# Turning the second product round: weights stationary, 448 tokens moving, output transposed, and two late terms

## The chip, the cores and the metric

The kernel runs on one core of a Trainium2 chip. The metric is the device time of one launch in microseconds; three runs gave 1165.35 to 1166.55, median 1165.88.

The core's engines work from queues of their own: PE (TensorE, the matmuls; PEld is its loading of weights), DVE (VectorE), ACT (ScalarE), POOL (GpSimd) and SP (SyncE, which issues most DMAs). An engine works through its queue in the order in which the instructions were written, and they wait for each other by semaphores. Each core has a small memory PSUM, into which matmuls add up; its banks are handed out from pools.

## The reference

Attention with a sigmoid in place of the softmax, then a product with `w_in`, a function of each element, and a product with `w_out`:

```python
scores = scale * np.matmul(q, k.transpose(0, 1, 3, 2)) - np.log(S)
attn = 1.0 / (1.0 + np.exp(-scores))
x = np.matmul(attn, v)          # (8, 12, 448, 64), then x: (3584, 768)
h = x @ w_in                    # (768, 2048)
g = h - np.tanh(h)
out = g @ w_out                 # (2048, 768)
```

There are 8 batches of 448 tokens (S) and 12 heads of width 64. All inputs and the output are f32.

## The kernel before

Work goes by batches. For each batch there is attention for 12 heads in six pairs (method `stream`, L467 on: scores `sc`, L394; the sigmoid on ACT, `a`, L405; its split into two f16 parts, `ahl`, L411 on ACT and L412 on DVE; the product with v, `acc`, L425; its move to `x`, L437 or L439), then the first product (`moe1`, `ph`, L773) with the function `g` behind it, and the second product (`moe2`, L838). To keep the accuracy of f32 with f16 matmuls, an operand is split into a high and a low f16 part, and a product is the sum of three (`prods`: high x high, high x low, low x high).

The attention of batch b + 1 runs among the matmuls of the second product of batch b. For b of 1 and above the method `second` does this: `moe2` is a generator that yields after each f (one of 16 slices of 128 rows of `w_out`), and the list BLOCKS says behind how many such steps the next block of attention is written. The numbers 16, 32 and 48 are the ends of token tiles. Batch 1 has a list of its own (BLOCKS1) with the same number 16. For batch 0 the order is written out by hand: a string ORDER with one letter for each piece, in which P is a piece of the second product. There the weights `w_out` are still being loaded (`rawo`), measured (`stb` on ACT, L170, then the matmuls `wl`, L201), scaled and split (`wo`, L237 and L240) at the same time.

The second product before: `gs` holds g with its 2048 rows on partitions, so 128 tokens of it are the stationary operand and half of `w_out` (384 columns) moves. A batch has three tiles of 128 tokens with two halves each (288 matmuls of 384 columns, `po`, L857), and then 64 tokens left over (`por`, L905: 96 matmuls with 64 stationary columns, two of which go to the two halves of a bank's partitions). Finished tiles are scaled by `iK` and moved to `o` by ACT (L890; in batch 0 `oh`, L876) and DVE (L894), for one tile by ACT alone (L892), the remainder by DVE (`orem`, L914), and stored by SP (L850). The PSUM pool `mm` has two banks, and a new tile waits until the eviction of the tile that had its bank is done.

Of the kernel before, what the change touches and what calls it, by code (L numbers as in the profile page):

```python
# [10 lines left out]
F32 = mybir.dt.float32  # L11
# [3 lines left out]
AF = mybir.ActivationFunctionType  # L15
ALU = mybir.AluOpType
# [3 lines left out]
P = 128  # L20
D = 64
# [12 lines left out]
class Builder:  # L34
# [5 lines left out]
    ORDER = (  # L40
        "lurmlorumsrrsrrmmlussmvvrrssvvrlrssvvrrvruvlssrurssvvrrssvlrrsvvvursrsvs"
        "vrrssvrsrrvvvvRrRrRRRMrRRRnRrRRGMRRwtMttRtRBtwRRtMwBgttMtRtRttMBttRtRttM"
        "tMBBtRttRMtBttMttMtRxtRtBRAtMtttAMtBttMttAttAttMMtAtPPtaRPRBPtBbtCaBCBAC"
        "PtFCCPBPCPPBZPPPCSBCPPBZCBCPPCCBPCCCSZBPPCCCPCXBaaAPaPPPBAPPaaaBBSPPSPSZ"
        "PSZSPPPPPPPSPBPPPZPPPNPZPSPZPSSNNPPSZPPZSSPPPPPPPPPPPP"
    )

    BLOCKS = (8, 11, 16, 20, 20, 20, 27, 32, 36, 36, 36, 43, 48, 52, 52)
# [242 lines left out]
    def w_out_scale(self, e):  # L291

        V = self.nc.vector
        self.w_out_bound(e)
        m = self.bound[e]
        total = self.sm.tile([P, 1], F32, name="wtot2")
        V.scalar_tensor_tensor(total, m, 1.05, m, op0=ALU.mult, op1=ALU.mult)
        S, inv = self.scale_of(total, f"swo{e}")
        self.Swo.append(S)
        V.tensor_copy(self.iSwo[:, e : e + 1], inv)  # L300
        h = slice(e * D, (e + 1) * D)
        V.tensor_copy(self.iSwo[h, 2:3], inv[h])

    def split_w_out(self, e):
        for f in range(0, self.NF, 2):
# [531 lines left out]
    def moe2(self, b, gs):  # L837
        nc = self.nc  # L838
        S = self.S
        ks = self.ks  # L840
        iK = self.sm.tile([P, 3], F32, name="iK")
        n = 1 if b == 0 else 3
        nc.vector.tensor_scalar(iK[:, :n], self.iSwo[:, :n], self.iSg, None, op0=ALU.mult)
        H = self.HALF
        base = b * S
        prods = ((0, 0), (0, 1), (1, 0))
        last = (self.NF - 1, 2)

        def store(o, j0, n, cols, queue=nc.sync):
            queue.dma_start(self.out[base + j0 : base + j0 + n, cols], o)  # L850

        nt = S // P

        def products(po, tk, f, e):
            for n, (x, w) in enumerate(prods):
                for i in e:
                    nc.tensor.matmul(  # L857
                        po[i][:, :H],
                        gs[f // 2][:, x, f % 2, tk * P : (tk + 1) * P],
                        self.wo[:, i * self.NF + 2 * ks[f // 2] + f % 2, w],  # L860
                        start=(f == 0 and n == 0),
                        stop=((f, n) == last),
                    )

        if b == 0:
            for e in range(2):
                for tk in range(nt):
                    po = {e: self.ps.tile([P, 512], F32, name="po", tag="mm", bufs=2)}
                    for f in range(0, self.NF, 2):
                        products(po, tk, f, (e,))  # L870
                        products(po, tk, f + 1, (e,))
                        if f + 2 == self.NF:
                            if (e, tk) == (1, 0):
                                nc.vector.tensor_scalar(iK[:, 1:], self.iSwo[:, 1:], self.iSg, None, op0=ALU.mult)
                            o = self.op.tile([P, H], F32, name="oh", tag="o", bufs=2)
                            nc.scalar.activation(o, po[e][:, :H], AF.Copy, scale=iK[:, e : e + 1])  # L876
                            store(o, tk * P, P, slice(e * H, (e + 1) * H))
                        yield 980
        else:
            for tk in range(nt):  # L880
                if b + 1 == self.B and tk % 2:
                    both = self.ps.tile([P, 2, 512], F32, name="po", tag="sc", bufs=2)
                    po = [both[:, e] for e in range(2)]
                else:
                    po = [self.ps.tile([P, 512], F32, name=f"po{e}", tag="mm", bufs=2) for e in range(2)]
                for f in range(self.NF):
                    products(po, tk, f, (0, 1))
                    if f == self.NF - 1:
                        o = self.op.tile([P, self.DM], F32, name="o", tag="o", bufs=2)
                        nc.scalar.activation(o[:, :H], po[0][:, :H], AF.Copy, scale=iK[:, 0:1])  # L890
                        if (b, tk) == (1, 0):
                            nc.scalar.activation(o[:, H:], po[1][:, :H], AF.Copy, scale=iK[:, 1:2])  # L892
                        else:
                            nc.vector.tensor_scalar(o[:, H:], po[1][:, :H], iK[:, 1:2], None, op0=ALU.mult)  # L894
                        store(o, tk * P, P, slice(0, self.DM))
                    yield 980
        nm = nt * P
        if b + 2 < self.B:
            po = self.ps.tile([P, 512], F32, name="por", tag="mm", bufs=2)
        else:  # L900
            po = self.ps.tile([P, 2, 512], F32, name="por", tag="sc", bufs=2)[:, 0]
        for f in range(self.NF):
            for n, (x, w) in enumerate(prods):
                for e in range(2):
                    nc.tensor.matmul(  # L905
                        po[e * D : (e + 1) * D, :H],
                        gs[f // 2][:, x, f % 2, nm:S],
                        self.wo[:, e * self.NF + 2 * ks[f // 2] + f % 2, w],
                        start=(f == 0 and n == 0),
                        stop=((f, n) == last),  # L910
                    )
            yield 560
        o = self.op.tile([P, H], F32, name="orem", tag="o", bufs=2)
        nc.vector.tensor_scalar(o, po[:, :H], iK[:, 2:3], None, op0=ALU.mult)  # L914
        for e in range(2):
            queue = nc.scalar if e and b + 1 == self.B else nc.sync
            store(o[e * D : (e + 1) * D], nm, S - nm, slice(e * H, (e + 1) * H), queue)


    def build(self):  # L920
        nc, tc = self.nc, self.tc

        def const(name, value, n=1):
            t = self.const.tile([P, n], F32, name=name)
            nc.vector.memset(t, value)
            return t

        self.nls = const("nls", -math.log(self.S))
        self.b1 = const("b1", B1)
        self.b2 = const("b2", B2)  # L930
        self.b3 = const("b3", -CUT * CUT)
        self.tiny = const("tiny", TINY)
        self.ih0 = const("ih0", 1.0)
        self.ihk0 = const("ihk0", KAPPA)
        self.iSwo = const("iswo", 1.0, 3)
        self.sums = [const(f"ss{i}", 0.0, 6) for i in range(2)]
        self.Swo = []
        self.sums_out, self.bound = [[], []], [None, None]
        self.xs32, self.x2b = False, []
        pieces = list(self.pieces())  # L940
        nA = 4 * self.NC
        E = mybir.EngineType
        with tc.manual_schedule(engines={E.PE, E.Activation, E.DVE, E.Pool}):
            nB = nA + self.NF + self.EARLY
            self.stage = tc.alloc_tile_pool(name="stage", bufs=2, reuse_waits="tile")
            self.blocks = self.stream()
            self.first(
                self.convert(pieces[:nA], "attention"),
                self.convert(pieces[nA:nB], "mixture"),
                self.convert(pieces[nB:], "product"),  # L950
            )
        with tc.manual_schedule(engines={E.PE, E.Activation, E.DVE, E.Pool, E.SP}):
            for b in range(1, self.B):
                self.batch(b)
        self.gp.release()
# [128 lines left out]
    def second(self, b, blocks, alone, events):  # L1084

        step = lambda: next(self.blocks)
        events += [(p, step) for p in blocks]
        scales = []

        def norms():  # L1090
            scales.append(self.batch_scales(self.xs, False))
            next(scales[0])

        if blocks:
            end = blocks[alone]
            events.append((end + 3, norms))
            events += [(p, lambda: next(scales[0], None)) for p in (end + 5, end + 7)]
        events.sort(key=lambda e: e[0])
        full = self.NF * (self.S // P)
        for k, _ in enumerate(self.moe2(b, self.gs)):  # L1100
            now = k + 1 if k < full else full + (k + 1 - full) / 2
            while events and events[0][0] <= now:
                events.pop(0)[1]()
        assert not events
# [34 lines left out]
```

## Time and profile before

| | |
|---|---|
| Median of the three runs | 1165.88 us |
| The profiled execution | 1166.29 us |
| Its span, first to last instruction | 1164.5 us |
| PE busy | 1153.1 us |
| DVE busy | 907.7 us |
| ACT busy | 865.5 us |
| Idle of PE in front of `po` (L857) | 3.1 us in all |
| Mean granted TensorE clock | 0.999 |

Busy times are those of one execution. The profile's chain of work follows the execution back from its last instruction, at each step to what released it; its pieces add up to the span. In the timeline a row is a run of instructions of one kind with its start, its length, the engine, the line, and in brackets the idle time in front of it with what ended it. Matmuls overlap in their pipeline, so the time of one in the queue is that of a long run divided by its count.

### The profile page before, as it was taken

Reading aid. Unit: us, or ns where it says so; the run is one execution under the profiler, and the core shown is the slowest. Engines: PE = TensorE matmul, PEld = TensorE weight load, DVE = VectorE, ACT = ScalarE, POOL = GpSimd, SP = SyncE. Lnnn points to the kernel's source line nnn. Section 1 sums busy time; section 2 is a strip of 40 time slices with the busy share of each in tenths; the row PEclk is TensorE's granted clock in tenths of the full one; section 3 lists DMA queues with packets and bytes.
Section 4 is the critical chain, followed back from the end, with each engine's and each line's share of the span. In section 5 each row is a group of like instructions: output and inputs, shape, how many; then the busy total and the mean of one; then the engine's idle time right before and its main releaser. Section 6 shows DMA issues by size and latency. Waiting matters only on the chain.

```text
span 1164.5 us, 18896 instructions
## 1 busy us (share of the span) xinstructions
PE 1153.1 (99%) x7563; PEld 597.4 (51%) x7564; DVE 907.7 (78%) x1308; ACT 865.5 (74%) x1195; POOL 79.1 (7%) x58
## 2 busy tenths in 40 slices
PE   9999999999999999999999999999999999999998
PEld 3345444555555555555555555555555555555565
DVE  6999999789777996679867897778976798646930
ACT  7988996588976888768887688867887688745820
POOL 0000000000120002200021000200022000300000
PEclk9999999999999999999999999999999999999999
DMA  9942171000222002210022101210012100000000
GB/s 358 357 163 64 42 224 53 29 7 1 80 75 64 7 1 78 62 53 1 17 76 62 40 1 31 82 58 24 1 55 84 53 1 9 23 28 7 1 14 35
DMA packets 34056, 70.43 MB, mean 60 GB/s; under 512 B 3888, under 2 KB 21040, under 8 KB 33968
## 3 DMA queue, kind: packets, MB, share of 16 engines
q1 hardware_dynamic: 33744, 68.89, 18.1%
q8 instruction: 59, 0.97, 0.4%
q10 hardware_dynamic: 224, 0.33, 0.1%
q14 instruction: 29, 0.24, 0.1%
HBM read 58.20 MB, written 11.01 MB: 59 GB/s over the span
## 4 chain that ended last, share of the span: by engine, by line
PE 73%; ACT 1%; issue 0%; DVE 0%; ACTq 0%
PE ph L773 28%; PE po L857 27%; PE sc L394 6%; PE acc L425 6%; PE por L905 5%; ACT a L405 0%; ACT ahl L411 0%; PE nm L690 0%; ACT sqn L335 0%; ACT x L439 0%; ACT Q L369 0%; DVE orem L914 0%; PE pbn L344 0%; ACT x L454 0%; ACT o L892 0%
## 5 line engine op out<-in xcount | busy, mean ns | idle before, releaser
L857 PE MATMUL po<-wo,g 128*128 128x384 f16 x2304 | 389.1, 326 | 3.1 <-DVE wo L240 1.6
L773 PE MATMUL ph<-xhl,wi 128*128 128x448 f16 x2016 | 382.6, 352 | 0.0
L857 PEld LDWEIGHTS <-g 128*128 128x128 f16 x2304 | 220.3, 98 | 170.1 <-issue 26.4
L773 PEld LDWEIGHTS <-wi 128*128 128x128 f16 x2016 | 196.7, 98 | 185.0 <-issue 2.1
L412 DVE SCALAR_TENSOR_TENSOR ahl<-a,ahl 128x896 f16<-128x896 f32 x126 | 162.7, 1326 | 125.6 <-ACT ahl L411 125.0
L405 ACT ACTIVATE a<-sc,nls,rn 128x896 f32<-128x896 f32 x147 | 155.8, 1090 | 37.4 <-PE sc L394 37.2
L811 ACT ACTIVATE u<-ph,ih 128x896 f32<-128x896 f32 x64 | 64.4, 1006 | 75.8 <-PE ph L773 74.0
L411 ACT ACTIVATE ahl<-a 128x896 f16<-128x896 f32 x126 | 113.2, 941 | 0.6
L394 PE MATMUL sc<-Q,K 64*128 64x448 f16 x1008 | 100.8, 353 | 0.9 <-DVE th L816 0.7
L815 DVE SCALAR_TENSOR_TENSOR m<-ph,ihk,u 128x896 f32<-128x896 f32 x64 | 73.5, 1149 | 25.6 <-ACT th L813 25.2
L766 ACT ACTIVATE g<-m,Sg 128x896 f16<-128x896 f32 x64 | 66.7, 1041 | 35.5 <-DVE m L829 28.5
L829 DVE COPY_PREDICATED m<-u,th 128x896 f32<-128x896 uint32 x64 | 77.2, 1206 | 6.8 <-ACT u L828 0.8
L425 PE MATMUL acc<-ahl,vhl 128*64 128x448 f16 (+1 forms) x864 | 80.6, 356 | 0.4 <-ACT tn L346 0.4
L456 POOL TENSOR_TENSOR x<-x 128x448 f32<-128x448 f32 x24 | 28.3, 1178 | 762.1 <-ACT x L439 762.1
L767 DVE SCALAR_TENSOR_TENSOR g<-m,Sg,g 128x896 f16<-128x896 f32 x64 | 73.4, 1147 | 6.8 <-ACT g L766 6.7
L826 DVE SCALAR_TENSOR_TENSOR m<-q,m 128x896 f32<-128x896 f32 x64 | 69.9, 1092 | 6.7 <-DVE m L822 0.5
L983 PE MATMUL ph<-x,wi 128*128 128x448 f32 x192 | 73.8, 540 | 0.0
L816 DVE SCALAR_TENSOR_TENSOR th<-ph,ih,th 128x896 f32<-128x896 f32 x64 | 73.3, 1145 | 0.0
L822 DVE SCALAR_TENSOR_TENSOR m<-q,m 128x896 f32<-128x896 f32 x64 | 69.6, 1087 | 0.0
L828 ACT ACTIVATE u<-u,b 128x896 f32<-128x896 f32 x64 | 66.7, 1042 | 1.9
L821 ACT ACTIVATE q<-u,b 128x896 f32<-128x896 f32 x64 | 65.8, 1028 | 0.0
L825 ACT ACTIVATE q<-u,b 128x896 f32<-128x896 f32 x64 | 65.8, 1028 | 0.0
(141 smaller groups left out, 1087.7 us busy)
## 6 DMA issues: line engine op xcount, KB each, us to landing
knn<-k SPq DMA_DIRECT2D x45, 224.0 KB, 2.6
qnn<-q SPq DMA_DIRECT2D x44, 224.0 KB, 2.6
rawo<-moe_w_out SPq DMA_DIRECT2D x22, 384.0 KB, 5.2
out<-o SPq DMA_DIRECT2D x21, 384.0 KB, 2.3
raw<-moe_w_in SPq DMA_DIRECT2D x13, 512.0 KB, 8.2
vn<-v SPq DMA_DIRECT2D x24, 256.0 KB, 2.8
wo<-moe_w_in SPq DMA_DIRECT2D x11, 512.0 KB, 8.3
vn<-v SPq DMA_DIRECT2D x24, 192.0 KB, 2.4
```

The lines of the kernel that those rows point to most:

```text
L394: self.nc.tensor.matmul(ps[i * m : (i + 1) * m, h, : self.S], K[i][r, w, c * P : c * P + m], Q[i][r, x, :], start=(n == 0), stop=(n == len ...
L405: self.nc.scalar.activation(a[:, 0], ps[:, :, : self.S], AF.Sigmoid, bias=self.nls, scale=scale)
L411: nc.scalar.activation(A[:, 0], a[:, 0], AF.Copy, scale=A_SCALE)
L412: nc.vector.scalar_tensor_tensor(A[:, 1], a[:, 0], A_SCALE, A[:, 0], op0=ALU.mult, op1=ALU.subtract)
L425: self.nc.tensor.matmul(acc[i][h * D : (h + 1) * D, : self.S], v[k, w, 2 * QT + h if half else h * QT + c], A[k, x, h], start=(n == 0 and ...
L767: nc.vector.scalar_tensor_tensor(g[:, 1], m, Sg, g[:, 0], op0=ALU.mult, op1=ALU.subtract)
L773: self.nc.tensor.matmul(ph, self.wi[:, self.slot(c, k), part, e * P : (e + 1) * P], xhl[c][:, x, :], start=(i == 0), stop=(i == len(prods) ...
L815: V.scalar_tensor_tensor(m, ps, ihk, u, op0=ALU.mult, op1=ALU.mult)
L816: V.scalar_tensor_tensor(th, ps, ih, th, op0=ALU.mult, op1=ALU.subtract)
L829: V.copy_predicated(m, u.bitcast(U32), th)
L857: nc.tensor.matmul(po[i][:, :H], gs[f // 2][:, x, f % 2, tk * P : (tk + 1) * P], self.wo[:, i * self.NF + 2 * ks[f // 2] + f % 2, w], star ...
L983: nc.tensor.matmul(ph[:, e, :S], self.fp32(self.wi, self.slot(c, k))[:, 0, e * P : (e + 1) * P], xs[c], start=(c == 0), stop=(c == self.NC ...
```

## The change

The operands of the second product change places. A slice of 128 columns of `w_out` is stationary and all 448 tokens of a batch move, so that the result is a block of 128 output columns by 448 tokens: six row blocks d, each of 16 f and three products, 288 matmuls a batch, and no remainder. The kernel's output is (768, 3584); the host turns it back. Blocks with even d are evicted by DVE and those with odd d by ACT, in batch 0 and for d = 0 of batch 1 all by ACT; the last block of the last batch is halved between ACT and DVE and goes out by two queues. The constant `iSwo` loses its third column with the copies into it.

For batches 1 to 7 the order of the terms changes too: d0 and d1 with f 0 to 13 each, then f 14 and 15 of d0, then f 14 and 15 of d1, then d2 to d5. `second` counts a step of f as 7/12 of one before (448 columns once, where it was 384 columns twice), so 28 steps count as 16. ORDER for batch 0 loses 16 letters P. Lines of unchanged code below move up by two.

```diff
         "vrrssvrsrrvvvvRrRrRRRMrRRRnRrRRGMRRwtMttRtRBtwRRtMwBgttMtRtRttMBttRtRttM"
-        "tMBBtRttRMtBttMttMtRxtRtBRAtMtttAMtBttMttAttAttMMtAtPPtaRPRBPtBbtCaBCBAC"
-        "PtFCCPBPCPPBZPPPCSBCPPBZCBCPPCCBPCCCSZBPPCCCPCXBaaAPaPPPBAPPaaaBBSPPSPSZ"
-        "PSZSPPPPPPPSPBPPPZPPPNPZPSPZPSSNNPPSZPPZSSPPPPPPPPPPPP"
+        "tMBBtRttRMtBttMttMtRxtRtBRAtMtttAMtBttMttAttAttMMtAtPPtaRRBPtBbtCaBCBACP"
+        "tFCCPBPCPPBZPPCSBCPPBZCBCPPCCBPCCCSZBPCCCPCXBaaAPaPPPBAPaaaBBSPPSPSZPSZS"
+        "PPPPPPSPBPPZPPPNPZPSPZSSNNPPSZPZSSPPPP"
...
+        def products(po, d, f):
+            e, at = d // half, d % half * P
             for n, (x, w) in enumerate(prods):
...
+                nc.tensor.matmul(
+                    po[:, :S],
+                    self.wo[:, e * self.NF + 2 * ks[f // 2] + f % 2, w, at : at + P],
+                    gs[f // 2][:, x, f % 2],
+                    start=(f == 0 and n == 0),
+                    stop=((f, n) == last),
+                )
+
+        def out(po, d):
+            iv = iK[:, d // half : d // half + 1]
+            rows = slice(d * P, (d + 1) * P)
+            o = self.op.tile([P, S], F32, name="o", tag="o", bufs=2)
+            if b + 1 == self.B and d == self.NC - 1:
+                h = S // 2
+                nc.scalar.activation(o[:, :h], po[:, :h], AF.Copy, scale=iv)
+                nc.scalar.dma_start(self.out[rows, b * S : b * S + h], o[:, :h])
+                nc.vector.tensor_scalar(o[:, h:], po[:, h:S], iv, None, op0=ALU.mult)
+                nc.sync.dma_start(self.out[rows, b * S + h : (b + 1) * S], o[:, h:])
+                return
+            if b == 0 or d % 2 or (b, d) == (1, 0):
+                nc.scalar.activation(o, po[:, :S], AF.Copy, scale=iv)
+            else:
+                nc.vector.tensor_scalar(o, po[:, :S], iv, None, op0=ALU.mult)
+            nc.sync.dma_start(self.out[rows, cols], o)
+
+        held = 2
+        order = [(d, f) for d in range(self.NC) for f in range(self.NF)]
+        if b:
+            late = range(self.NF - held, self.NF)
+            order = [(d, f) for d in range(2) for f in range(self.NF - held)]
+            order += [(d, f) for d in range(2) for f in late]
+            order += [(d, f) for d in range(2, self.NC) for f in range(self.NF)]
+        po = {}
+        for d, f in order:
+            if f == 0:
+                po[d] = self.ps.tile([P, 512], F32, name="po", tag="mm", bufs=2)
+            products(po[d], d, f)
+            if f == self.NF - 1:
+                if (b, d) == (0, half):
+                    nc.vector.tensor_scalar(iK[:, 1:], self.iSwo[:, 1:], self.iSg, None, op0=ALU.mult)
+                out(po.pop(d), d)
+            if b or f % 2:
+                yield 567
...
-            now = k + 1 if k < full else full + (k + 1 - full) / 2
+            now = (k + 1) * 7 / 12
...
-    shape = (B * S, H * D)
+    shape = (H * D, B * S)
...
-    return r.results[0]["out"]
+    return np.ascontiguousarray(r.results[0]["out"].T)
```

What this does to the order on ACT, at three places. The first is batch 3's second product at the attention block numbered 16; `a32` is the sigmoid's output, `sqn` the squares of q, k and v of a later pair, `o` the eviction of a finished tile. ACT's queue before:

```order
L411 ACTIVATE ahl_5970<-a32_5942 128x896
L335 ACTIVATE sqn_5977,ss1_116<-vn_5321 128x512
L335 ACTIVATE sqn_5979,ss1_116<-vn_5323 128x384
L890 ACTIVATE o_6011<-po0_5824,iK_5822 128x384
L405 ACTIVATE a32_6035<-sc_6015,nls_98,rn_5242 128x896
L405 ACTIVATE a32_6037<-sc_6022,nls_98,rn_5242 128x896
L335 ACTIVATE sqn_6039,ss1_116<-knn_5973 128x448
L335 ACTIVATE sqn_6041,ss1_116<-qnn_5975 128x448
L411 ACTIVATE ahl_6043<-a32_6035 128x896
L411 ACTIVATE ahl_6046<-a32_6037 128x896
```

And after the change, where `po_5608` is the row block d1:

```order
L409 ACTIVATE ahl_5668<-a32_5640 128x896
L333 ACTIVATE sqn_5675,ss1_116<-vn_5059 128x512
L333 ACTIVATE sqn_5677,ss1_116<-vn_5061 128x384
L403 ACTIVATE a32_5726<-sc_5706,nls_98,rn_4980 128x896
L403 ACTIVATE a32_5728<-sc_5713,nls_98,rn_4980 128x896
L333 ACTIVATE sqn_5730,ss1_116<-knn_5671 128x448
L333 ACTIVATE sqn_5732,ss1_116<-qnn_5673 128x448
L409 ACTIVATE ahl_5734<-a32_5726 128x896
L409 ACTIVATE ahl_5737<-a32_5728 128x896
L871 ACTIVATE o_5755<-po_5608,iK_5529 128x448
```

The eviction moved from ahead of the block's six instructions to behind them. PE's queue after the change, where the late terms of d1 end and d2 (`po_5758`) begins:

```order
L851 MATMUL po_5608<-g_5521,wo_97 128x448
L851 LDWEIGHTS wo_97
L851 MATMUL po_5608<-g_5521,wo_97 128x448
L851 LDWEIGHTS wo_97
L851 MATMUL po_5758<-g_5121,wo_97 128x448 [waits Activation_49]
```

The first matmul of d2 follows the last one of d1 at once, and the wait that it carries is for the count of ACT that `o_5755` gives, since d2 takes d1's bank; so it is in batches 2 to 6. In batch 1 it is the count of the eviction of d0, which is on ACT there and directly ahead of that of d1, and in batch 7 that of d0 on DVE.

The third place is batch 0, ACT's queue around the end of d1. Before:

```order
L170 ACTIVATE stb<-rawo 128x384
L876 ACTIVATE oh<-po,iK 128x384
L170 ACTIVATE stb<-rawo 128x384 x2
L405 ACTIVATE a_1556<-sc,nls,rn 128x896
L369 ACTIVATE K<-knn,sn 128x448
L369 ACTIVATE Q<-qnn,sn 128x448
```

After:

```order
L170 ACTIVATE stb<-rawo 128x384 x2
L237 ACTIVATE wi<-wi,swi_s 128x2x256
L403 ACTIVATE a_1592<-sc,nls,rn 128x896
L403 ACTIVATE a_1594<-sc,nls,rn 128x896
L435 ACTIVATE x_1602<-acc 128x448
L452 ACTIVATE x_1604<-x_1602 128x448
L333 ACTIVATE sqn,ss_116<-vn 128x512
L333 ACTIVATE sqn,ss_116<-vn 128x384
L871 ACTIVATE o<-po,iK 128x448
```

A piece P is now 448 columns by six matmuls instead of 384 by six, the blocks end at other letters, and the eviction of d1 comes later in ACT's queue, behind the squares of v. The first matmul of d2 waits for it there too.

More of the change, by code (lines that the diff above doesn't have):

```diff
@@ L300, in w_out_scale @@
         V.tensor_copy(self.iSwo[:, e : e + 1], inv)
-        h = slice(e * D, (e + 1) * D)
-        V.tensor_copy(self.iSwo[h, 2:3], inv[h])
     def split_w_out(self, e):
@@ L840, in moe2 @@
         ks = self.ks
-        iK = self.sm.tile([P, 3], F32, name="iK")
-        n = 1 if b == 0 else 3
+        iK = self.sm.tile([P, 2], F32, name="iK")
+        n = 1 if b == 0 else 2
         nc.vector.tensor_scalar(iK[:, :n], self.iSwo[:, :n], self.iSg, None, op0=ALU.mult)
         H = self.HALF
-        base = b * S
+        cols = slice(b * S, (b + 1) * S)
         prods = ((0, 0), (0, 1), (1, 0))
         last = (self.NF - 1, 2)
-        def store(o, j0, n, cols, queue=nc.sync):
-            queue.dma_start(self.out[base + j0 : base + j0 + n, cols], o)
@@ L852, in moe2 @@
-        nt = S // P
-        def products(po, tk, f, e):
+        half = self.NC // 2
+        def products(po, d, f):
+            e, at = d // half, d % half * P
             for n, (x, w) in enumerate(prods):
[L856 to L917, printed above, removed]
+                nc.tensor.matmul(
[5 more added lines that the diff above has]
+                )
@@ L934, in build @@
         self.ihk0 = const("ihk0", KAPPA)
-        self.iSwo = const("iswo", 1.0, 3)
+        self.iSwo = const("iswo", 1.0, 2)
         self.sums = [const(f"ss{i}", 0.0, 6) for i in range(2)]
@@ L1098, in second @@
         events.sort(key=lambda e: e[0])
-        full = self.NF * (self.S // P)
         for k, _ in enumerate(self.moe2(b, self.gs)):
-            now = k + 1 if k < full else full + (k + 1 - full) / 2
+            now = (k + 1) * 7 / 12
             while events and events[0][0] <= now:
```

## The prediction

> **What bounds the kernel now.** I read the page first, then the chain of work that ended last over the final 120 us, then the timeline of all engines around the places where the second product's banks are handed over. On the page:
>
> ```profile
> PE 1153.1 (99%) x7563; PEld 597.4 (51%) x7564; DVE 907.7 (78%) x1308; ACT 865.5 (74%) x1195; POOL 79.1 (7%) x58
> ...
> PE 73%; ACT 1%; issue 0%; DVE 0%; ACTq 0%
> PE ph L773 28%; PE po L857 27%; PE sc L394 6%; PE acc L425 6%; PE por L905 5%; ACT a L405 0%; ACT ahl L411 0%; PE nm L690 0%; ACT sqn L335 0%; ACT x L439 0%; ACT Q L369 0%; DVE orem L914 0%; PE pbn L344 0%; ACT x L454 0%; ACT o L892 0%
> ```
>
> PE is busy for 99% of the span, and nearly all of the chain is matmuls. So there are two ways to move the time: fewer or dearer columns on PE, or pauses of PE. There are hardly any pauses now, so a change can add many and remove few. The end of the chain gives the prices (start, us, what, count), first for the last batch, then for batch 3:
>
> ```profile
> 1051.09 54.59 PE ph L773 x288
> 1105.68 46.80 PE po L857 x288
> 1152.48 7.94 PE por L905 x96
> 1160.42 0.02 issue
> 1160.44 0.62 DVE orem L914
> ```
>
> ```profile
> 633.71 4.02 PE por L905 x48
> ```
>
> A `po` matmul (384 columns) costs 46.80/288 = 0.1625 us of the queue, a `ph` matmul (448 columns) 54.59/288 = 0.1896 us. The longer means of single instructions on the page overlap each other; these quotients are what counts.
>
> **The change part by part.**
>
> *Columns.* Before, a batch's second product is 288 matmuls of 384 columns and 96 of the remainder, which run in pairs. After, it is 288 of 448 columns, f16, 128x128 stationary: the form of `ph` exactly. Batches 1 to 6, with the remainder in two parts of 4.02: (46.80 + 8.04) - 54.59 = 0.25 us saved each, **-1.5**. Batch 7: 54.74 - 54.59, **-0.15**. So the turning itself is worth almost nothing; PE had little to lose in the remainder. The weight loads stay under the matmuls, as these do (mean 98 ns under 0.19 us):
>
> ```profile
> L773 PEld LDWEIGHTS <-wi 128*128 128x128 f16 x2016 | 196.7, 98 | 185.0 <-issue 2.1
> ```
>
>
> *Batches 2 to 6: the hand-over at d2.* Only two banks hold results (`mm`, 2 buffers). Before, the attention block due at 16 fell right behind a token tile's last matmul and its eviction stood ahead of the block's softmax on ACT: PE computed scores while ACT freed the bank. The rows of batch 3 (start, us, engine, line):
>
> ```profile
> 582.27 0.58 ACT L890 ACTIVATE o<-po,iK 128x384 f32<-128x384 f32 x1 [0.35 <-PE po L857]
> ...
> 583.12 2.09 ACT L405 ACTIVATE a<-sc,nls,rn 128x896 f32<-128x896 f32 x2 [0.26 <-DVE ahl L412]
> ...
> 585.10 0.57 ACT L335 ACTIVATE sqn<-knn 128x448 bf16<-128x448 f32 x1
> ...
> 586.22 1.78 ACT L411 ACTIVATE ahl<-a 128x896 f16<-128x896 f32 x2
> ```
>
> and the same place in the chain:
>
> ```profile
> 582.40 1.36 PE sc L394 x18
> 583.76 4.01 PE po L857 x24
> ```
>
> Now the block falls before the twelve late matmuls of d0 and d1. Its softmax, squares and splits enter ACT's queue first; the eviction of d1 comes behind them, and d2's first matmul waits for that eviction, since d2 takes d1's bank. On this row's clock PE has the scores done at 583.76 and the twelve at 583.76 + 12 x 0.1896 = 586.03. ACT has not been relieved: `a` cannot start earlier (it waited for DVE, not for the eviction), so the splits end at 586.22 + 1.78 = 588.00. An eviction of 448 columns is not in the trace on this line; the nearest rows are these:
>
> ```profile
> L439 ACT ACTIVATE x<-acc,rn x36: 620/634/635, 296.3 to 1037.9; 128x448 f32<-128x448 f32 x36
> ```
>
> It overlaps the split by about 0.1 us and takes 0.63, so it ends at 588.53; with 0.04 for PE's start (the issue row of batch 1 below shows that much) d2 begins at 588.57. The pause is 588.57 - 586.03 = 2.5 us. Bounds: not below 1.9 (ending with the splits), not above 3.2 (one more eviction ahead). Five batches: **+12.7**, 9.5 to 16. Queued behind the waiting matmul is everything of PE; DVE and the attention of the next block have nothing to give that PE could do meanwhile. DVE's eviction of d0, later still, isn't what d2 waits for, and d3 needs its bank only 48 matmuls (9.1 us) further on. The store of d1 waits on SP for that eviction, and loads of k and q are queued behind it:
>
> ```profile
> knn<-k SPq DMA_DIRECT2D x45, 224.0 KB, 2.6
> ```
>
> They land 2.6 us after issue; a store that is 2.5 us late delays their users only together with PE, which is as late, so I cost that at nothing.
>
> *Batch 1.* ACT is saturated here and both evictions were on it:
>
> ```profile
> 307.17 1.43 PE L394 MATMUL sc<-Q,K 64*128 64x448 f16 x18
> ...
> 307.98 0.20 ACT L335 ACTIVATION_READ_ACCUMULATOR sqn<-vn 128x1 f32 x1
> 308.07 0.57 ACT L890 ACTIVATE o<-po,iK 128x384 f32<-128x384 f32 x1
> ...
> 308.54 0.58 ACT L892 ACTIVATE o<-po,iK 128x384 f32<-128x384 f32 x1
> ...
> 309.00 2.09 ACT L405 ACTIVATE a<-sc,nls,rn 128x896 f32<-128x896 f32 x2
> ...
> 312.08 1.80 ACT L411 ACTIVATE ahl<-a 128x896 f16<-128x896 f32 x2
> ```
>
> ```profile
> 309.12 0.04 issue
> 309.16 3.90 PE po L857 x23
> ```
>
> A pause exists already: scores end at 307.17 + 1.36 = 308.53, `po` resumes at 309.16, 0.63. After, `a` moves up by 0.9 to 308.1, the splits end at 313.88 - 0.9 = 312.98, the eviction of d0 (for which d2 waits here) at 313.5. PE is ready at 308.53 + 2.27 = 310.80. The pause is 2.75 less the 0.63 that it replaces: **+2.1**.
>
> *Batch 0.* The order string has 48 product letters in place of 64 and moves them. The eviction of d1 now stands behind two `stb`, `wi`, two `a`, an `x` and its square and the two squares of `vn`. These do not move, since the first `stb` is released by the last `acc` matmul:
>
> ```profile
> 173.75 0.56 ACT L170 ACTIVATE stb<-rawo 128x384 f32<-128x384 f32 x1 [0.48 <-PE acc L425]
> ...
> 178.93 0.19 ACT L335 ACTIVATION_READ_ACCUMULATOR sqn<-vn 128x1 f32 x1
> ```
>
> ```profile
> 173.68 2.12 PE L857 MATMUL po<-wo,g 128*128 128x384 f16 x12
> 175.64 0.67 PE L201 MATMUL wl<-stb,onesb 128*128 128x384 bf16 x3
> ```
>
> Behind 173.68 PE has six matmuls of d1 (1.14) and three of `wl` (0.5 of the queue), and is ready for d2 at 175.4 to 175.7. ACT reaches the eviction at 179.0, done at 179.65. A pause of about 4.0. Part of it is paid back: PE's present waits in this stage are for work that goes on during the pause.
>
> ```profile
> PE po L857 <- DVE wo L240: 1.6, 3, 0.6
> ...
> PE sc L394 <- ACT a L405: 0.2, 1, 0.2
> ```
>
> 4.0 - 1.6 - 0.2 - 0.25 (columns) = **+2.0**. Bounds: -1 (if ACT runs ahead and the pause is 1 us), +3.8 (nothing paid back).
>
> *Tail.* `orem`'s 0.62 becomes two halves of 224 columns on two engines. Through these two lengths,
>
> ```profile
> L890 ACT ACTIVATE o<-po,iK 128x384 f32<-128x384 f32 x21 | 12.2, 581 | 56.8 <-PE po L857 56.8
> ```
>
> 581 ns for 384 and 634 for 448, a line gives 0.45: **-0.17**. In batch 7 there is no attention, the twelve late matmuls take 2.27 us, and d0's eviction on DVE (at most 0.63) is done in the 1.14 us of d1's late six: no pause.
>
> Sum against the profiled execution: 1166.29 - 1.5 - 0.15 + 12.7 + 2.1 + 2.0 - 0.17 = **1181.3**.
>
> *The clock.* So far PE never stood still long enough to lose its clock. What a pause does is seen only at the two ends (windows: PEclk is the third figure from the end; then the warming matmuls):
>
> ```profile
> 1162.50:1163.00 0.50, 0.00 (x0) 0.00 (x0) 0.00 (x0) 0.00 (x0) 0.00 (x0) 0.87 0.86 258
> 1163.00:1163.50 0.50, 0.00 (x0) 0.00 (x0) 0.00 (x0) 0.00 (x0) 0.00 (x0) 0.50 0.04 9
> ```
>
> ```profile
> 1.20 3.60 PE L97 MATMUL warm<-onesb 128*128 128x512 bf16 x8 [1.20 <-DVE nls L925]
> ```
>
> The share 0.87 puts the drop to 0.50 at 1162.87, 2.45 us after the last matmul. The eight warming matmuls took 0.45 us each; at `ph`'s rate 512 columns take 0.217, so a spell of half clock costs 8 x 0.233 = 1.9 us. All seven new pauses are 2.5 to 4.0 long, so each may set off a spell: between 0 and 7 x 1.9 = 13.3. One drop at 2.45 us does not say that 2.5 always suffices: five of the pauses lie at that very edge, batch 1's a little beyond, batch 0's well beyond. I take batch 0's and one of the other six, **+3.7**: 1185.0. The profiled execution stands 0.4 above the median of 1165.88, so the forecast is **1184.6**.
>
> The Trainium skill, "TensorE: Matmul & The Clock Gate", section "What's actually happening", says that the gate falls to half after a whole idle window of about 3.4 us, the windows running freely. By that alone only batch 0's pause is long enough, and the sum would be 1181.3 + 1.9 - 0.4 = 1182.8; the trace agrees only in part, since its drop came 2.45 us after the last matmul, so that a partly busy window seems to count as well.
>
> **Rivals.** *The waits come, the clock stays.* 1181.3 - 0.4 = 1180.9. For it: 2.5 us barely reaches the one interval seen. *Only the longest pause slows the clock*, if a standstill must last longer than the 2.75 us of batch 1: one spell, 1181.3 + 1.9 - 0.4 = 1182.8. For it: 4.0 is far beyond the interval seen, the others are not. (This is the case that the skill's rule gives.) *Part of the pauses is covered.* If DVE frees `a`'s buffers earlier or batch 0's ACT runs ahead, half of the 16.8 us goes: about 1172.5, 1171 to 1178 with a spell. Against it: ACT's queue is fixed, and its times hang on scores and DVE splits that don't move. *Not slower: ACT's chain fits beneath the twelve matmuls.* Place: d2's start in batches 1 to 6. It decides at 3.63 us from the block's first score matmul to the end of d1's eviction; what I read is 6.17. If it fits, only the savings remain: 1166.29 - 1.5 - 0.15 - 0.17 - 0.4 = 1164.1, and 0.6 less with batch 1's old pause gone. Against it: `a` and `ahl` alone are 2.09 + 1.78 = 3.87. *The clock falls at every pause, or another bank waits too:* 1190 to 1195. *The new form isn't `ph`'s form in price:* each 1% on a `po` matmul is 8 x 54.6 x 0.01 = 4.4 us; against it is that shape, type and load are the same.
>
> **How the numbers follow.** Waits with two to four spells, 1184 to 1189: 0.40. Waits without: 0.25. With the one of batch 0: 0.12. Partly covered: 0.12. Fits: 0.06. All spells or more waits: 0.05. The predicted time is the first's, 1184.6. The range of 1174 to 1191 holds the first three, most of the fourth and the start of the last; about 0.12 is left out. A measurement can tell about 0.2% (2.3 us) from no change. Only the case that fits lies inside or below that bound, half and half: faster 0.03, within 0.03, slower 0.94.
>
> **What would show it.** Right: in batches 2 to 6 PE idle some 2.5 us at the start of d2, released by ACT's eviction, with the splits just ahead of it; some 2.7 in batch 1 and 4 in batch 0; none in batch 7; a batch of `po` at 54.6 without attention; the clock at half for a few us behind some of the pauses. Wrong: no waits on the eviction, a matmul interval other than 0.19 us, or a pause at d3 or d4.

## The result, and the profile after

| | before | after |
|---|---|---|
| Median of five runs | 1165.88 us | 1182.76 us |
| All runs | 1165.27 to 1167.96 | 1182.12 to 1185.99 |
| Ratio, with 95% interval | | 1.0148 (1.0130 to 1.0165) |
| Profiled execution, its span | 1166.29, 1164.5 | 1182.76, 1181.0 |
| Mean granted TensorE clock | 0.999 | 0.996 |

The change makes the kernel 1.5% slower; 1184.6 was forecast. The page of the changed kernel (engines' busy time, the chain of work by engine and line, and the group of the turned product):

```profile
PE 1154.3 (98%) x6795; PEld 555.6 (47%) x6796; DVE 901.6 (76%) x1299; ACT 866.2 (73%) x1195; POOL 75.3 (6%) x58
...
PE 71%; ACT 4%; issue 0%; DVE 0%; ACTq 0%
...
L851 PE MATMUL po<-g,wo 128*128 128x448 f16 x2304 | 455.9, 355 | 18.0 <-ACT o L871 18.0
```

PE is as long busy as before (1154.3 against 1153.1), though with 768 matmuls fewer. What is new stands at the end of the third line: 18.0 us in which PE stood still in front of `po` for the eviction on ACT, where before it was 3.1 for other reasons. In the chain ACT's share goes from 1% to 4%. PE's waits of the changed kernel (us in total, times, longest):

```profile
PE po L851 <- ACT o L871: 18.0, 7, 3.5
PE pbn L342 <- ACT sqn L333: 1.7, 2, 0.9
PE sc L392 <- DVE th L814: 1.4, 1, 1.4
```

Seven waits, one in each of batches 0 to 6. The place in batch 3 that the prediction worked through, in the timeline and then in the chain:

```profile
588.99 1.43 PE L392 MATMUL sc<-Q,K 64*128 64x448 f16 x18
590.36 2.44 PE L851 MATMUL po<-g,wo 128*128 128x448 f16 x12
595.23 1.86 PE L851 MATMUL po<-g,wo 128*128 128x448 f16 x9 [2.43 <-ACT o L871]
```

```profile
589.78 2.09 ACT a L403 x2
...
592.23 0.75 ACT sqn L333 x3
592.98 1.68 ACT ahl L409 x2
594.65 0.53 ACT o L871
595.19 0.04 issue
595.23 1.86 PE po L851 x9
```

The chain leaves PE at the block's first scores, runs through ACT's softmax, squares and splits to the eviction of d1, and comes back to PE at d2: the twelve late matmuls (the second row of the timeline) lie beside it and cover less than half.

By stages, from the start of one batch's first product to the next (us; the pieces `PE ph` of the chain give the starts):

| stage | before | after | difference |
|---|---|---|---|
| start of the second product of batch 0 | 129.55 | 128.55 | -1.0 |
| from there to `ph` of batch 1 | 96.72 | 98.60 | +1.9 |
| `ph` of batch 1 to `ph` of batch 2 | 144.64 | 148.01 | +3.4 |
| batches 2, 3, 5, 6, each | 137.35 (6: 130.76) | 139.58 (6: 132.99) | +2.2 |
| batch 4 | 137.36 | 141.13 | +3.8 |
| batch 7 to the last matmul's end | 109.33 | 108.97 | -0.4 |

Together with 0.1 less behind the last matmul that is the 16.5 us by which the span grew. Batch 4 has the same wait as batches 3 and 5 and is 1.5 us longer: there, and in batches 0 and 1, the clock fell (windows; PEclk is the third figure from the end):

```profile
178.00:178.50 0.50, 0.43 (x2) 0.25 (x2) 0.46 (x2) 0.01 (x1) 0.00 (x0) 0.70 0.00 0
178.50:179.00 0.50, 0.50 (x3) 0.15 (x1) 0.41 (x1) 0.00 (x0) 0.00 (x0) 0.50 0.20 75
...
181.50:182.00 0.50, 0.50 (x12) 0.17 (x12) 0.42 (x3) 0.12 (x1) 0.00 (x0) 0.89 0.00 0
...
314.50:315.00 0.50, 0.50 (x3) 0.25 (x3) 0.50 (x1) 0.41 (x1) 0.00 (x0) 0.73 0.00 0
...
318.00:318.50 0.50, 0.50 (x8) 0.28 (x6) 0.39 (x3) 0.01 (x1) 0.00 (x0) 0.86 0.00 0
```

From 178.20 to 181.61 and from 314.73 to 318.14 PE runs at half clock, 3.41 us each time.

### The profile page after: what moved, and what is told of

The parts are those of the page before. It is cut to its first block, busy times and chain, and to the rows that moved or that the text cites. A ratio compares the mean times of both kernels' runs of the same rounds, so it can differ in the third digit from the quotient of the medians.

```text
span 1181.0 us, 17374 instructions
## 1 busy us (share of the span) xinstructions
PE 1154.3 (98%) x6795; PEld 555.6 (47%) x6796; DVE 901.6 (76%) x1299; ACT 866.2 (73%) x1195; POOL 75.3 (6%) x58
## 4 chain that ended last, share of the span: by engine, by line
PE 71%; ACT 4%; issue 0%; DVE 0%; ACTq 0%
PE po L851 31%; PE ph L771 28%; PE acc L423 6%; PE sc L392 6%; ACT a L403 1%; ACT ahl L409 1%; ACT sqn L333 1%; ACT o L871 0%; PE nm L688 0%; ACT x L437 0%; ACT Q L367 0%; ACT x L452 0%; ACT o L865 0%; DVE o L867 0%; PE pbn L342 0%
## 5 line engine op out<-in xcount | busy, mean ns | idle before, releaser
L851 PE MATMUL po<-g,wo 128*128 128x448 f16 x2304 | 455.9, 355 | 18.0 <-ACT o L871 18.0
L851 PEld LDWEIGHTS <-wo 128*128 128x128 f16 x2304 | 220.5, 98 | 246.0 <-issue 50.9
L410 DVE SCALAR_TENSOR_TENSOR ahl<-a,ahl 128x896 f16<-128x896 f32 x126 | 159.1, 1298 | 140.5 <-ACT ahl L409 139.8
L454 POOL TENSOR_TENSOR x<-x 128x448 f32<-128x448 f32 x24 | 24.7, 1029 | 782.2 <-ACT x L437 782.2
```

The lines of the kernel that those rows point to most:

```text
L410: nc.vector.scalar_tensor_tensor(A[:, 1], a[:, 0], A_SCALE, A[:, 0], op0=ALU.mult, op1=ALU.subtract)
L851: nc.tensor.matmul(po[:, :S], self.wo[:, e * self.NF + 2 * ks[f // 2] + f % 2, w, at : at + P], gs[f // 2][:, x, f % 2], start=(f == 0 and ...
```

## The experiments

The theory: the pause at d2 is the queue on ACT (or DVE) in front of the eviction, made by the late terms in batches 1 to 6 and by a letter of ORDER in batch 0. The main rival: the turned form as such, six blocks on two banks with 448-wide evictions and no block of attention behind most of them, makes the wait. The runs of the kernel before, beside these, had medians of 1166.06 (first four) and 1166.34 (last four).

**The late terms undone.**

```diff
-        held = 2
+        held = 0
```

> Only the late placement is undone: d0 and d1 of batches 1 to 7 run f 0 to 15 in one go, all else as in the changed kernel. Theory: the pause at d2 (2.42 us in batches 1 to 6) exists because the evictions of d0 and d1 stand behind the softmax of block 16 in the queues of ACT and DVE. Without late terms d0 is evicted by DVE long before and d2 takes d0's bank, so the pause at d2 is gone in batches 1 to 6. But the last slices of g end 11.1 us after the batch's start in the trace of the changed kernel (580.35 against 569.22) and d0's f14 now wants them after 14 x 0.567 + 0.7 = 8.6 us: a new pause of 2 to 2.5 us there in batches 2 to 7, released by the last g on ACT and DVE. Total 1178 to 1185, little gained. Batch 0 keeps its 3.5 us. Rival (the turned form with its two banks makes the pause, whatever the order): the pauses at d2 stay at 2.4, 1182 to 1187.

Measured: 1183.48 us (1182.13 to 1185.5), ratio 1.0151 (1.0136 to 1.0166). The time is that of the changed kernel, the waits are others. PE's waits, and the place in batch 3:

```profile
PE po L851 <- ACT g L764: 9.0, 6, 2.0
PE po L851 <- DVE g L765: 3.9, 6, 0.6
PE po L851 <- ACT o L871: 3.7, 1, 3.7
```

```profile
577.32 0.54 PE L851 MATMUL po<-g,wo 128*128 128x448 f16 x2 [1.39 <-ACT g L764]
...
578.51 3.71 PE L851 MATMUL po<-g,wo 128*128 128x448 f16 x10 [0.65 <-DVE g L765]
```

No wait for an eviction is left but that of batch 0, so the turned form with its two banks isn't the cause in batches 1 to 6. In exchange PE waits for the last slices of g in batches 2 to 7, in two pieces of 1.39 and 0.65. So the late terms do something: a row block of 448 tokens wants f14 after 14 steps of 0.57 us, where a token tile before wanted it after 14 of 0.98. They buy 2 us at d0's end and pay 2.4 at d2's start. Short as they are, these waits cut the clock too: the profiled execution, the slowest of the four, shows half clock in batches 0, 2, 3, 6 and 7.

**The late terms sooner.** d0's two late terms behind d1's f9, and d1 without late terms.

```diff
+            cut = self.NF - 3 * held
-            order = [(d, f) for d in range(2) for f in range(self.NF - held)]
-            order += [(d, f) for d in range(2) for f in late]
+            order = [(0, f) for f in range(self.NF - held)]
+            order += [(1, f) for f in range(cut)]
+            order += [(0, f) for f in late]
+            order += [(1, f) for f in range(cut, self.NF)]
```

> d0's two late terms stand behind d1's f9 instead of behind d1's f13, and d1 has no late terms of its own: d0 is complete two steps before block 16, and its eviction ahead of the block's softmax. Theory: d2 takes d0's bank, already free, and the six pauses of 2.42 us in batches 1 to 6 vanish with the clock spells behind two of them (1.5 us each); g's last slices are ready by then. 1182.8 - 14.5 - 3.1 = 1165, 1163 to 1167; batch 0 keeps its pause. Rival (turned form with two banks): pauses at d2 stay, 1182 or more. Rival (the late terms only hide a wait for g): a pause of some 2 us at f14 of d0 takes their place, 1178 to 1182.

Measured: 1163.9 us (1163.45 to 1165.85), ratio to the kernel before 0.9981 (0.9972 to 0.9991). The one wait for an eviction that is left is batch 0's:

```profile
PE po L851 <- ACT o L871: 3.1, 1, 3.1
```

Batch 3, PE: scores of block 16, then d1's last twelve matmuls and d2's first nine without a gap.

```profile
581.63 1.43 PE L392 MATMUL sc<-Q,K 64*128 64x448 f16 x18
583.00 4.15 PE L851 MATMUL po<-g,wo 128*128 128x448 f16 x21
```

The same terms at another place: both the wait for g and the wait for the eviction are gone, and with the six waits the slowdown. A stage of batches 2 to 5 takes 137.00 us, 0.35 less than before the change. That is what the turning itself is worth.

**The letter of batch 0.** The 16th P, which ends d1, ahead of the block B.

```diff
-        "tFCCPBPCPPBZPPCSBCPPBZCBCPPCCBPCCCSZBPCCCPCXBaaAPaPPPBAPaaaBBSPPSPSZPSZS"
+        "tFCCPBPCPPBZPPCSBCPPBZCBCPPCCBPCCCSZPBCCCPCXBaaAPaPPPBAPaaaBBSPPSPSZPSZS"
```

> Only ORDER: the 16th letter P (the end of d1 and its eviction) is put ahead of the block B before it, so that the eviction stands ahead of that block's six instructions on ACT. Theory: batch 0's pause of 3.47 us and the spell of half clock behind it (1.6) go, while DVE's wo waits (1.6 before the change) may come back in part: 1177.7 to 1180.5. Rival (batch 0's pause is covered anyway by those waits): 1182 to 1183, the wo waits of 1.6 back in full and the pause only moved.

Measured: 1179.6 us (1178.78 to 1183.29), ratio 1.0123 (1.0105 to 1.0140). The waits for ACT's eviction fall from seven to six, and smaller ones come in batch 0 behind it:

```profile
PE po L851 <- ACT o L871: 14.6, 6, 2.4
...
PE sc L392 <- ACT a L403: 1.2, 1, 1.2
```

Batch 0's stage is 95.54 us, 1.2 shorter than before the change. DVE's `wo` waits did not come back.

**DVE evicts d1** from batch 2 on. The edit reaches batch 7 as well, which the expectation leaves out; no wait came there.

```diff
-            if b == 0 or d % 2 or (b, d) == (1, 0):
+            if b == 0 or (d % 2 and (b < 2 or d != 1)) or (b, d) == (1, 0):
```

> In batches 2 to 6 d1 is evicted by DVE instead of ACT; nothing else. Theory (the pause is the queue ahead of the eviction): DVE's two splits of the block end later than ACT's, at 595.94 against 594.66 in batch 3, so that d2 starts about 1.3 to 1.4 us later: pauses of 3.7 to 3.9, released by DVE, 5 x 1.35 = +6.8, and one to three more spells of half clock: 1190 to 1194. Rival (the eviction's own length decides, 0.62 on ACT and 0.68 on DVE): the same within 0.5 us, 1182 to 1186.

Measured: 1199.02 us (1198.27 to 1199.99), ratio 1.0281 (1.0264 to 1.0298). The waits came as foretold, the time is 5 us above the range:

```profile
PE po L851 <- DVE o L873: 18.9, 5, 3.8
PE po L851 <- ACT o L871: 5.8, 2, 3.4
```

Five waits of 3.8 where they were 2.4, so it is the queue ahead of the eviction that sets them; by its own length (0.68 against 0.62) nothing would have moved. What was mis-sized is the clock. It fell behind all seven pauses, and for twice as long in batches 3 to 6; batch 3:

```profile
598.00:598.50 0.50, 0.00 (x0) 0.00 (x0) 0.50 (x2) 0.03 (x1) 0.00 (x0) 0.98 0.00 0
598.50:599.00 0.50, 0.00 (x0) 0.00 (x0) 0.50 (x1) 0.00 (x0) 0.00 (x0) 0.50 0.00 0
605.00:605.50 0.50, 0.50 (x6) 0.04 (x2) 0.46 (x2) 0.50 (x1) 0.00 (x0) 0.69 0.00 0
```

Half clock from 598.49 to 605.31, 6.83 us, 5.4 of them with work: 2.7 lost in place of 1.5.

**Both repairs together**: the diffs of the second and third experiments.

> The sooner late terms and the moved letter of batch 0 together. Theory: the two gains are of different places and add up; from 1163.9 batch 0's stage goes from 97.2 us to the 95.5 that it took with the letter alone: 1162.2, 1161.5 to 1163. Rival (batch 0's gain was in good part the spell of half clock, which the sooner kernel does not have in its profile): 1163.5 to 1164.

Measured: 1161.7 us (1161.17 to 1162.16), ratio 0.9960 (0.9947 to 0.9972). The gains add up, and this version is faster than both kernels: 0.4% under the one before. No wait of PE for an eviction is left in its profile.

**The pauses filled.** The changed kernel with matmuls that nobody reads between d1 and d2.

```diff
                 out(po.pop(d), d)
+                if d == 1 and b + 1 < self.B:
+                    fill = self.ps.tile([P, 2, 512], F32, name="fill", tag="sc", bufs=2)
+                    for i in range(12 if b else 18):
+                        nc.tensor.matmul(
+                            fill[:, 0, :S],
+                            self.wo[:, 2 * ks[f // 2] + f % 2, 0, :P],
+                            gs[f // 2][:, 0, f % 2],
+                            start=True,
+                            stop=True,
+                        )
```

> The changed kernel with 12 extra matmuls (18 in batch 0) between d1 and d2 in batches 0 to 6, into a scores bank, read by nobody: PE has work in the pause, and the pause itself stays. Theory (spells of half clock come from the pauses' idleness and cost 1.5 each, three in the profile): without them 1182.8 - 4.5 = 1178.3, 1177.5 to 1180, granted clock 1.00 throughout, and the runs lie closer together. Rival (the clock costs nothing that matters): 1182 to 1184. If the filling matmuls lengthen the pause, by waiting for their bank: over 1184, to be seen as a wait in front of them.

Measured: 1179.19 us (1178.89 to 1180.36), ratio 1.0113 (1.0098 to 1.0129), granted clock 1.000. Batch 3:

```profile
588.03 2.44 PE L851 MATMUL po<-g,wo 128*128 128x448 f16 x12
590.31 2.43 PE L895 MATMUL fill<-g,wo 128*128 128x448 f16 x12
592.90 1.86 PE L851 MATMUL po<-g,wo 128*128 128x448 f16 x9 [0.16 <-ACT o L871]
```

The filling takes the place of the idle time, and d2 starts 4.87 us behind the start of the late terms, as without it (590.36 to 595.23). The kernel is 3.6 us faster for work that it doesn't need, which is the price of the clock in this kernel's median.

**The block later.** Block 16 behind the late terms, with its scores as cover for d1's eviction.

```diff
-    BLOCKS = (8, 11, 16, 20, 20, 20, 27, 32, 36, 36, 36, 43, 48, 52, 52)
+    BLOCKS = (8, 11, 18.5, 20, 20, 20, 27, 32, 36, 36, 36, 43, 48, 52, 52)
...
-    BLOCKS1 = (4, 7, 8, 11, 13, 16, 20, 20, 20, 27, 32, 36, 36, 36, 43, 48, 52, 52)
+    BLOCKS1 = (4, 7, 8, 11, 13, 18.5, 20, 20, 20, 27, 32, 36, 36, 36, 43, 48, 52, 52)
```

> The changed kernel with block 16 put at 18.5, behind the late terms of d1, so behind both evictions in the queues and with its scores as cover. Theory: no wait at d2 in batches 1 to 6 and no spell there; but the next block's norms now come 3 steps later instead of 7, and PE reaches its pbn some 3.1 us after the block's first score where ACT has the squares ready after 4.0 to 4.5: a pause of about 1 us there, too short for a spell. 1182.8 - 6 x 2.4 - 3.1 + 6 x 1 = 1171, 1167 to 1174. Rival (it is the turned form with its two banks): 1182 or more with waits at d2.

Measured: 1174.27 us (1172.8 to 1174.94), ratio 1.0066 (1.0052 to 1.0080). The wait at d2 is gone, and the chain of the next block is what waits now (batch 3):

```profile
593.53 0.17 PE L342 MATMUL pbn<-ss,onesb 128*128 128x6 bf16 x1 [0.79 <-ACT sqn L333]
...
595.36 2.58 PE L423 MATMUL acc<-ahl,vhl 128*64 128x448 f16 x30 [0.43 <-ACT tn L344]
```

1.2 us in two pieces, a little more than foretold, and with batch 0's pause of 3.6 left in place the time lies just above the expected range; the stage of batch 3 takes 138.45 against 137.00 with the terms sooner.

**The old form with the fault.** The kernel before, unturned, with the block 16 one step sooner, so that the evictions of a token tile come behind its softmax.

```diff
-    BLOCKS = (8, 11, 16, 20, 20, 20, 27, 32, 36, 36, 36, 43, 48, 52, 52)
+    BLOCKS = (8, 11, 15, 20, 20, 20, 27, 32, 36, 36, 36, 43, 48, 52, 52)
...
-    BLOCKS1 = (4, 7, 8, 11, 13, 16, 20, 20, 20, 27, 32, 36, 36, 36, 43, 48, 52, 52)
+    BLOCKS1 = (4, 7, 8, 11, 13, 15, 20, 20, 20, 27, 32, 36, 36, 36, 43, 48, 52, 52)
```

> The kernel before, unturned, with the block numbered 16 put at 15, so that the tile's last six matmuls and both evictions come behind the block's softmax. Theory (the order makes the pause, not the turned form): the next tile waits for ACT's and DVE's evictions, 1.36 + 0.98 us after the block's first score PE is ready, DVE's eviction ends some 7.6 us after it: pauses of 4 to 5.3 in batches 1 to 6, with a spell or two windows of half clock behind each (1.5 to 2.7): 1166 + 6 x 4.8 + 6 x 2.2 = 1208, 1198 to 1215. Rival (pauses belong to the turned form): within 3 us of the kernel before, 1165 to 1169.

Measured: 1208.48 us (1208.14 to 1208.72), ratio 1.0361 (1.0347 to 1.0375). PE's waits:

```profile
PE po L857 <- ACT o L890: 23.1, 6, 4.8
PE po L857 <- DVE o L894: 5.0, 5, 1.0
```

4.7 us a batch for the same mistake in the old form. So it is the order that makes the wait, whichever operand is stationary.

## Why the prediction was right, point by point

*The hand-over at d2, batches 2 to 6.* Right in kind, place, releaser and size: 2.42 us each against 2.54. The second, fourth and eighth experiments show the cause: with d0's eviction ahead of the block the wait is gone, with a longer queue ahead of it the wait grows by that queue, and it can be made in the old form. A pause costs the stage slightly more than its row, 2.23 + 0.35 = 2.58 (the stage's difference and what it gains without the pause), since PE counts as busy until its last matmul has left the pipeline (0.355 us for one on the page, against 0.19 of the queue). One step of the working was wrong and cost nothing: it held that `a` waits for DVE. In the changed kernel DVE's splits were done at 589.27, and ACT had stood idle for 1.67 us when the block's scores released `a` at 589.78. That is 0.79 us behind the first score, as before the change (582.33 to 583.12), so the pause kept its size by luck.

*Batch 1.* 2.42 by its row, 2.58 with the pipeline's end, where 2.75 was expected: `a` started 0.78 us behind the first score (308.20 to 308.98), not 0.93.

*Batch 0.* The pause came, 3.47 for 4.0, but its net price was mis-sized: +2.0 was forecast, and in the second experiment, where no spell falls into it, the stage takes 97.23, +0.5. Two steps failed. That ACT's instructions "do not move" was wrong. Counted from the start of the second product, which came 1.0 us sooner in this execution, the pair of `stb` begins as before (172.70 - 129.55 = 43.15, 171.68 - 128.55 = 43.13). But the second of the two follows at once, where ACT stood still for 0.48 us before, and the squares end 0.6 us sooner (179.12 - 129.55 = 49.57, 177.50 - 128.55 = 48.95). Why that wait is gone isn't shown. And what is paid back was read from the idle rows, 1.6 for the three `wo` waits; by the matmuls' starts and rates they cost 2.4 (182.69 + 0.16 to 183.51, 183.51 + 0.98 to 185.22, 191.64 + 5.04 to 197.71), since the idle row begins only when the pipeline is empty. The prediction also had no term for the waits ahead of that place: the one at `pbn` grew from 0.38 to 1.56 us in the second experiment and two for g (0.44 and 0.69) went, which came to 0.3 in all.

*Columns.* -0.35 a batch where -0.25 and -0.15 were forecast. 0.11 of it lies in `ph`, whose 288 matmuls take 54.48 in place of 54.59 behind the turned product; why wasn't tried.

*Tail.* -0.1 for -0.17. The halves took 0.45 us each, as worked out, but one behind the other:

```profile
1177.01 0.03 ACTq L865
1177.03 0.05 issue
1177.08 0.46 ACT o L865
1177.54 0.02 issue
1177.56 0.45 DVE o L867
```

*The clock.* Three spells in the profile where two were taken. They cost 1.5 us in batch 4, 1.6 in batch 1 (148.01 against the 146.37 of the same stage in the third experiment, where the clock did not fall in it) and 1.4 in batch 0 (98.60 against 97.23), where 1.9 was taken. The filled pauses put the whole at 3.6 us in the median, for a forecast of 3.7. That the two lie so close is partly luck: too few spells at too high a price, and a number that was chosen between none and seven. The spell taken as surest, that of batch 0, did not come in the second experiment's profile, though its pause there was 3.06 us. The rivals of an undisturbed clock (1180.9) and of a single spell (1182.8, which was also the sum by the rule of the Trainium skill) are decided by the profile and not by the time, which lies on the second: three of seven pauses cut it.

*The sum* was 2.2 us high against the profiled execution (1185.0 for 1182.76). Batch 0 gave 1.5 of it, the start of the program 1.0 (a chance; the second product of batch 0 starts between 128.55 and 130.71 in the profiles here), the other batches and the tail some 0.5. The clock took 0.8 back, 4.5 for 3.7.

*Not slower* fell where it was put: the eviction's end lay 6.2 us behind the block's first score (588.99 to 595.18), far over 3.63. No wait came at d3 to d5 or in batch 7.

## What to carry to other kernels

When a term of a product is put off, its tile's eviction is put off too; look what enters the evicting engine's queue in between, and whose bank the next tile takes. The cover has to be as long as that queue, not as long as the eviction: here 2.3 us of matmuls stood against 4.9 us of softmax, squares and splits on ACT. A term may be late enough for its operand and still early enough for the eviction; try the places between before paying for either end.

## What the hardware showed that was not expected

The clock falls at moments of a fixed grid. In the profile of the changed kernel it fell at 178.20, 314.73 and 734.57, which are 40 and 123 steps of 3.413 us apart, and each spell lasted one step. In another execution the grid lies elsewhere: a fall in the profile of the first experiment, at 438.54, is 76.3 steps from 178.20. The third fall of the changed kernel:

```profile
734.50:735.00 0.50, 0.19 (x1) 0.10 (x1) 0.50 (x2) 0.26 (x1) 0.00 (x0) 0.57 0.00 0
...
738.00:738.50 0.50, 0.50 (x6) 0.21 (x6) 0.00 (x0) 0.23 (x1) 0.00 (x0) 1.00 0.45 165
```

By that grid equal pauses are unequal. Batch 4's pause (732.39 to 734.81) put 2.18 us, 64%, into the step that ended at 734.57, and the clock fell. Batch 3's (592.80 to 595.23) put at most 1.82, 53%, into a step (594.62 is a boundary), and it did not. The other profiles narrow this. In batches 2, 3, 6 and 7 of the first experiment, steps in which PE was busy for 1.36 to 1.45 us of 3.41 (58 to 60% idle) ended with a fall; in the second and third, steps with 1.48 and 1.41 (57 and 59% idle) did not. So in this kernel the boundary lies near 58% idle of one step, and these busy times do not give it more closely.

The Trainium skill, "TensorE: Matmul & The Clock Gate", section "What's actually happening", gives a free-running window of 3413 ns, and lets the gate fall after an idle window. The trace agrees with the window's length; but here a window counted as idle in which PE was busy for up to 42% of the time.

The clock comes back by another measure. Where it falls in the middle of a pause, as in batch 3 of the fourth experiment, the rest of the pause lies in the first step at half clock. That step was 43% idle (598.49 to 601.90, PE busy 1.94 us), less than cut the clock anywhere here, and yet half clock lasted a second step, 6.83 us in all. In the eighth experiment a step at half clock that was 30% idle (745.81 to 749.22) was followed by another, and one that was 20% idle (602.45 to 605.86) was not.
